# Softmax attention and gated GLU on one core: scores issued as jobs of one head and one key tile, in an order from an event model

## The chip, the cores and the metric

The kernel runs on one core of a Trainium2 chip. The metric is device time in microseconds: 1281.01 us before, the median of three runs (1276.12 to 1281.82). Engines: TensorE (PE, with its weight loads as PEld), VectorE (DVE), ScalarE (ACT), GpSimd (POOL), and SyncE (SP), which issues most DMAs.

## What is computed

x is 2048 x 640, in bf16. After a LayerNorm, 32 heads of width 20 attend over all 2048 tokens, and a GLU of inner width 1728 makes a gate for the result.

```python
    def _A_ref(x, wqkv, wo):
        B, S, D = x.shape
        H = 32; Dh = D // H
        qkv = (lambda x, *d: x.transpose(*d))((x @ wqkv).reshape(B, S, 3, H, Dh), 2, 0, 3, 1, 4)
        q, k, v = qkv[0], qkv[1], qkv[2]
        scale = Dh ** -0.5
        scores = jnp.einsum("bhqd,bhkd->bhqk", q, k) * scale
        p = _softmax(scores, axis=-1)
        o = jnp.einsum("bhqk,bhkd->bhqd", p, v)
        return (lambda x, *d: x.transpose(*d))(o, 0, 2, 1, 3).reshape(B, S, D) @ wo
    ...
    x = A_x
    xn = _layernorm(x, axis=-1)
    s = _A_ref(xn, A_wqkv, A_wo)
    g = _silu(_B_ref(xn, B_w_gate, B_w_up, B_w_down))
    return x + s * g
```

`_B_ref` is sigmoid(xn @ w_gate) * (xn @ w_up), times w_down.

## The kernel before

**Lead.** Four chunks of 512 tokens are normalised (statistics on VectorE, L217 to L223, the scaling on ScalarE, L227), transposed on TensorE (L232) into `xnT`, and K of the first head group is projected (L240, L241). After the fourth chunk the largest K is found over 2048 tokens (L136); then come the first Q and two of the six V pieces of the first pair of groups (L242 to L250).

**Blocks.** The rest is 32 blocks: 8 groups of 4 heads, times 4 chunks of 512 queries. A block has 16 key tiles times 4 heads, 64 score tiles of 128 keys x 512 queries, one PSUM bank each. 12 key tiles (`AKT`) go to ScalarE, which takes the exp of two heads in one instruction of two banks into a `pt` buffer (L549, L550; 6 buffers). 4 key tiles (`DKT`) go to VectorE, which builds the exponential in integers: one instruction clears two banks of `scD` to `iv` (L559), and four passes over `iv` make four tables `pb` (L567), each with its own scaled V (`vss`, made on GpSimd, L173). The four heads lie in four 32-row strips of TensorE, so score matmuls of different heads run side by side; PV matmuls (L456) write 21 rows for each head into strips of the one bank `oacc`. A PV round is four matmuls, one for each head: 12 + 4 x 4 = 28 rounds a block.

**PSUM.** Two slots `scA` of 2 banks, `scD` of 2, `oacc` 1, and one bank `misc` for all else: K, Q and V of the coming group, and the GLU (`item_k`, `item_q`, `item_v`, `item_gu`, `item_down`), at the end the output projection (`item_out`).

**Order.** The order on TensorE, ScalarE and VectorE is the program's own (`manual_schedule`); each engine runs its queue in that order. One step of the loop (L538) is one exp. After it come the VectorE instructions put off from earlier steps (`deferred`), the fill of the slot two steps ahead, and then either, on even steps, the matmuls of one whole step of an item (five for a projection), or up to four PV rounds from one queue over all heads. `norm` (L462) follows the last PV round of a block: VectorE copies `oacc` (L465), SyncE sends the sums to DRAM and back as `lt` (L467, L469), VectorE takes the reciprocal (L471) directly behind the copy in its queue, then `rd`, four broadcasts `rl`, GpSimd's product `on_bf` (L478) and the stores to `oU`. GLU items run in the first 28 blocks, output items (chunk by chunk, when a chunk of queries has gone through all groups) in the last three and behind the loop.

Of the kernel before, what the change touches and what calls it, by code (L numbers as in the profile page):

```python
# [18 lines left out]
P = 128  # L19
# [31 lines left out]
def kernel(  # L51
# [25 lines left out]

    def exp_act(o, i):
        zero = mybir.ImmediateValue(dtype=FP32, value=0.0)
        sc = mybir.ImmediateValue(dtype=FP32, value=exp_scale)  # L80
        return nc.scalar.add_instruction(mybir.InstActivation(  # L81
            func=ACT.Exp, name=nc.get_next_instruction_name(), engine=ENG.Activation,
            ins=[nc.scalar.lower_ap(i), zero, sc, zero], outs=[nc.scalar.lower_ap(o)]))
# [47 lines left out]
    def k_evac(ps, g, c):  # L131
        nc.vector.tensor_scalar(out=kTs[g % 2][:, c * 512:(c + 1) * 512], in0=ps,
                                scalar1=ones_r[:, 0:1], scalar2=None, op0=ALU.add)
        if c == S // 512 - 1:
# [29 lines left out]
    def v_evac(ps, pr, tts, eng=None):  # L164
# [3 lines left out]
        for i, tt in enumerate(tts):  # L168
            if tt in DKT:
                vf = wk.tile([P, 2 * GC], FP32, tag="vf", bufs=1, name="vf")  # L170
# [9 lines left out]
    with tc.tile_pool(name="ln", bufs=2) as lp, \  # L180
# [29 lines left out]

        for c in range(NQC):
# [8 lines left out]
            nc.scalar.activation(out=rstd, in_=mv[:, :, 1:2], func=ACT.Sqrt, bias=eps_t, scale=1.0)  # L220
            nc.vector.reciprocal(out=rstd, in_=rstd)
# [4 lines left out]
            for i in range(4):  # L226
                nc.scalar.activation(out=xn[:, i, :], in_=xt[:, i, :], func=ACT.Identity,  # L227
                                     bias=nb[:, i, :], scale=rstd[:, i, :])
            for kd in range(KD):
                tp = psP.tile([P, 4 * P], BF16, tag="tp", bufs=3, name="tp")  # L230
# [4 lines left out]
                if kd % 2 == 0:  # L235
                    nc.vector.tensor_copy(out=dst, in_=tp)
                else:
                    nc.scalar.copy(out=dst, in_=tp)
# [398 lines left out]
```

## Time and profile before

| | before |
|---|---|
| median of the runs | 1281.01 us |
| profiled execution | 1271.02 us |
| its span | 1269.3 us |
| TensorE busy | 975.9 us (77%) |
| VectorE busy | 867.4 us (68%) |
| ScalarE busy | 807.5 us (64%) |
| GpSimd busy | 98.7 us (8%) |
| DMA | 54.63 MB, mean 43 GB/s |
| mean granted TensorE clock | 0.887 |

The rows further down come from one profiled execution. Times are in us from the start of its span, unless marked ns. Matmuls are pipelined and their ends are modelled, so that TensorE's need is better read from the distance of starts than from its busy time. A wait is written as "who waited <- for whom". [...]

### The profile page before, as it was taken

What the parts mean: (1) busy time and instruction counts of PE and PEld (TensorE: products, weight loads), DVE (VectorE), ACT (ScalarE), POOL (GpSimd) and SP (SyncE); (2) the same over time, 40 slices, a digit from 0 to 9 for tenths busy, and PEclk for the clock granted to TensorE, in tenths of its full rate; (3) what the DMA queues carried; (4) which work ended last, traced back from release to release, by engine and by line L of the source; (5) the groups of instructions that cost most, each with busy time, mean ns of one, the idle gap of its engine ahead of it and who ended that gap; (6) DMA issues with size and microseconds to landing.
All of it is one profiled execution on the core that took longest, in us unless ns stands there. A gap on an engine that the chain in (4) does not pass through costs nothing. (4 is left out here: it accounts for less than half of the span.)

```text
span 1269.3 us, 19838 instructions
## 1 busy us (share of the span) xinstructions
PE 975.9 (77%) x7552; PEld 343.1 (27%) x7552; DVE 867.4 (68%) x1654; ACT 807.5 (64%) x918; POOL 98.7 (8%) x144
## 2 busy tenths in 40 slices
PE   4787787777877777877778778777877877777874
PEld 2322222323222222332222222332222222222222
DVE  6767776666756676667666766766775767577871
ACT  6567765556666666665577676656675766776750
POOL 2100000110000000011000000000100000002223
PEclk9889988889889898988899898889898998978885
DMA  6311111011121110001111110010111000002323
GB/s 174 103 47 38 41 38 34 23 32 47 33 53 34 28 48 27 19 23 30 51 31 34 41 38 25 17 31 24 53 33 28 13 22 27 19 14 73 95 76 105
DMA packets 85808, 54.63 MB, mean 43 GB/s; under 512 B 33552, under 2 KB 79440, under 8 KB 85712
## 3 DMA queue, kind: packets, MB, share of 16 engines
q1 hardware_dynamic: 84560, 52.05, 14.9%
q8 instruction: 59, 0.97, 0.3%
q10 hardware_dynamic: 1152, 1.31, 0.3%
q14 instruction: 37, 0.30, 0.1%
HBM read 42.32 MB, written 8.39 MB: 40 GB/s over the span
## 5 line engine op out<-in xcount | busy, mean ns | idle before, releaser
L81 ACT ACTIVATE pt<-scA_461 128x1024 bf16<-128x1024 f32 x384 | 397.0, 1034 | 232.0 <-PE oacc L456 223.7
L81 ACT ACTIVATE pt<-scA_462 128x1024 bf16<-128x1024 f32 x384 | 396.7, 1033 | 105.1 <-PE scA_462 L434 61.5
L567 DVE TENSOR_SCALAR pb<-iv 128x1024 int16<-128x1024 int16 x1024 | 383.5, 437 | 45.8 <-PE oacc L456 39.0
L559 DVE TENSOR_SCALAR iv<-scD 128x1024 int16<-128x1024 f32 x256 | 311.5, 1217 | 19.2 <-PE scD L434 18.6
L321 PE MATMUL mps<-xnT,wgu 128*128 128x512 bf16 (+1 forms) x560 | 155.5, 413 | 54.7 <-DVE hT L343 44.3
L434 PE MATMUL scA_461<-q,kT_70 32*128 32x512 bf16 x384 | 81.1, 415 | 47.0 <-ACT pt L81 46.8
L434 PE MATMUL scA_461<-q,kT_69 32*128 32x512 bf16 x384 | 77.6, 397 | 49.5 <-ACT pt L81 48.5
L434 PEld LDWEIGHTS <-kT_69 32*128 32x128 bf16 x1024 | 45.6, 91 | 204.6 <-issue 200.7
L434 PEld LDWEIGHTS <-kT_70 32*128 32x128 bf16 x1024 | 44.9, 92 | 198.9 <-issue 194.6
L478 POOL TENSOR_TENSOR on_bf<-on,rl 128x512 bf16<-128x512 f32 x32 | 41.8, 1307 | 712.4 <-DMA rl<-rd 636.6
L471 DVE RECIPROCAL rt<-lt 128x16 f32<-128x16 f32 x32 | 8.1, 253 | 122.9 <-DMA lt<-ld 122.9
L321 PEld LDWEIGHTS <-wgu 128*128 128x128 bf16 (+1 forms) x560 | 52.4, 103 | 128.2 <-issue 91.5
L434 PE MATMUL scA_462<-q,kT_70 32*128 32x512 bf16 x384 | 82.6, 426 | 5.3 <-ACT pt L81 5.0
L456 PE MATMUL oacc<-pt,v_72 128*21 128x512 bf16 x768 | 74.0, 404 | 16.1 <-DVE on L465 16.1
L355 PE MATMUL mps<-wd,hT 128*128 128x320 bf16 x448 | 77.6, 308 | 10.7 <-DVE gqs L371 10.1
L434 PE MATMUL scA_462<-q,kT_69 32*128 32x512 bf16 x384 | 79.1, 407 | 5.4 <-ACT pt L81 5.0
L456 PE MATMUL oacc<-pt,v_71 128*21 128x512 bf16 x768 | 70.5, 392 | 13.4 <-DVE on L465 13.4
L343 DVE SCALAR_TENSOR_TENSOR hT<-tnh,mps 128x512 bf16<-128x512 bf16 (+1 forms) x56 | 38.4, 685 | 60.7 <-PE mps L321 59.7
L456 PE MATMUL oacc<-pb,vs_74 128*21 128x512 bf16 x768 | 73.2, 433 | 0.0
L333 ACT ACTIVATE tnh<-mps 128x512 bf16<-128x512 f32 (+1 forms) x56 | 33.5, 599 | 60.3 <-PE mps L321 60.3
L456 PE MATMUL oacc<-pb,vs_73 128*21 128x512 bf16 x768 | 70.3, 417 | 0.0
L161 PE MATMUL mps<-wv,xnT 128*128 128x160 bf16 x290 | 34.5, 293 | 34.1 <-DVE vf L171 26.5
(84 smaller groups left out, 826.1 us busy)
## 6 DMA issues: line engine op xcount, KB each, us to landing
rl<-rd SPq DMA_DIRECT2D x128, 64.0 KB
wgu<-in_B_w_gate_dram SPq DMA_DIRECT2D x24, 320.0 KB
wgu<-in_B_w_up_dram SPq DMA_DIRECT2D x24, 320.0 KB
gq_dram<-gqs SPq DMA_DIRECT2D x32, 160.0 KB
gqr<-gq_dram SPq DMA_DIRECT2D x16, 320.0 KB
xr<-in_A_x_dram SPq DMA_DIRECT2D x16, 160.0 KB
out_dram<-ot SPq DMA_DIRECT2D x16, 160.0 KB
oU<-on_bf SPq DMA_DIRECT2D x112, 20.0 KB
```

The lines of the kernel that those rows point to most:

```text
L81: return nc.scalar.add_instruction(mybir.InstActivation(func=ACT.Exp, name=nc.get_next_instruction_name(), engine=ENG.Activation, ins=[nc. ...
L161: nc.tensor.matmul(ps[:, i * 2 * GC:(i + 1) * 2 * GC], lhsT=xnT[:, kd, tt * P:(tt + 1) * P], rhs=w[:, kd, :], start=(kd == 0), stop=(kd == ...
L321: nc.tensor.matmul(ps[0:fs, :], lhsT=w[:, i, kd, ko * P:ko * P + fs], rhs=xnT[:, kd, c * QC:(c + 1) * QC], start=(kd == 0), stop=(kd == KD ...
L333: nc.scalar.activation(out=st["t"][0:fs, :], in_=st["g"][0:fs, :], func=ACT.Tanh, scale=0.5)
L343: nc.vector.scalar_tensor_tensor(out=hT[0:fs, kf, :], in0=st["t"][0:fs, :], scalar=1.0, in1=st["u"][0:fs, :], op0=ALU.add, op1=ALU.mult)
L355: nc.tensor.matmul(st["ps"][:, 0:HD], lhsT=hT[0:fsz[kf], kf, t4 * P:(t4 + 1) * P], rhs=wd[0:fsz[kf], kf, h * HD:(h + 1) * HD], start=(kf = ...
L434: nc.tensor.matmul(sc[:, i, :], lhsT=kTs[(b_ // NQC) % 2][32 * j:32 * j + 32, kt_ * P:(kt_ + 1) * P], rhs=qs[b_][32 * j:32 * j + 32, :], s ...
L456: nc.tensor.matmul(oacc[32 * j:32 * j + DH + 1, :], lhsT=lhsT, rhs=rhs, start=(i == 0), stop=(i == tot - 1), tile_position=(0, 32 * j), sk ...
L471: nc.vector.reciprocal(out=rt, in_=lt)
L478: nc.gpsimd.tensor_tensor(out=on_bf, in0=on, in1=rl, op=ALU.mult)
L559: nc.vector.tensor_scalar(out=iv, in0=scD, scalar1=I_OFF, scalar2=I_LOW, op0=ALU.add, op1=ALU.max)
L567: nc.vector.tensor_scalar(out=pb[:, k, :, :].bitcast(I16), in0=iv, scalar1=0.25, scalar2=cst, op0=ALU.mult, op1=ALU.add)
```

## The change

The unit of work becomes a job: one head and one key tile, one bank of scores. ScalarE has a slot of three banks and one of two, filled and read in turn; VectorE has a slot of one bank, and its `iv` and `pb` tiles now hold all four heads of a key tile, so that clearing takes four instructions of 512 columns and a pass is one of 2048. `pt` becomes 3 buffers of 3 jobs and 4 of 2 (17 jobs where there were 12), `pb` 2 of 4 heads (3 of 2 before). Jobs are claimed when a slot is filled; when the ScalarE key tiles of a block are used up, ScalarE takes VectorE's that nobody has begun (`claim_act`).

The order comes from a small model that runs while the program is written: it keeps the time at which each engine is free, with fixed lengths for each kind of instruction, and issues on each engine the next thing that its model holds ready. On TensorE a fill goes first when ScalarE would starve, projections are issued matmul by matmul (M), and PV as rounds of one unit from each head's own queue; K, Q and V items go before GLU and output items. `norm` is cut in two: `norm_a` copies `oacc` and sends the sums, `norm_b` with the reciprocal is issued at least 7 us of model time later.

Smaller edits: half of the LayerNorm scaling goes to GpSimd, every K chunk has its own maximum (`k_max`), K evacuation in the lead is on ScalarE, the first Q is projected after the first chunk, the exp table is loaded by an exp after the last square root, all six V pieces of the first pair move into the loop, and the buffers of the output stage share the place of the GLU's down weights (`wd`). Tanh takes its scale as an immediate. The score, projection, evacuation and PV instructions are otherwise as before. Behind the loop `norm_b` of the last block and the output items that are left are issued in sequence.

Its core:

```diff
+    def k_evac(ps, g, c, on_act=False):
+        dst = kTs[g % 2][:, c * 512:(c + 1) * 512]
+        if on_act:
+            nc.scalar.activation(out=dst, in_=ps, func=ACT.Identity, bias=ones_r[:, 0:1], scale=1.0)
+        else:
+            nc.vector.tensor_scalar(out=dst, in0=ps, scalar1=ones_r[:, 0:1], scalar2=None, op0=ALU.add)
+
+    def k_max(g, c):
+        if c == 0:
+            mks[g] = wk.tile([P, NQC], FP32, tag="mk4", bufs=2, name="mk4")
+        nc.vector.tensor_reduce(out=mks[g][:, c:c + 1], in_=kTs[g % 2][:, c * 512:(c + 1) * 512],
+                                axis=AXISX, op=ALU.max, apply_absolute_value=True)
+        if c == NQC - 1:
             mk = wk.tile([P, 1], FP32, tag="mk", bufs=2, name="mk")
-            nc.vector.tensor_reduce(out=mk, in_=kTs[g % 2], axis=AXISX, op=ALU.max,
-                                    apply_absolute_value=True)
+            nc.vector.tensor_reduce(out=mk, in_=mks[g], axis=AXISX, op=ALU.max)
...
             k_mm(psk, 0, c)
-            k_evac(psk, 0, c)
-        psq = psP.tile([P, 512], FP32, tag="pq", bufs=1, name="psq")
-        q_mm(psq, 0, 0)
-        aq0 = q_abs(psq)
+            k_evac(psk, 0, c, on_act=True)
+            k_max(0, c)
...
-    scA = [psum.tile([P, 2, 512], FP32, name=f"scA{i}", tag=f"scA{i}") for i in range(2)]
-    scD = psum.tile([P, 2, 512], FP32, name="scD", tag="scD") if ND else None
+    SLOT = (3, 2)
+    scA = [psum.tile([P, n, 512], FP32, name=f"scA{n}", tag=f"scA{n}") for n in SLOT]
+    scD = psum.tile([P, 512], FP32, name="scD", tag="scD")
     oacc = psum.tile([P, QC], FP32, name="oacc", tag="oacc")
     nc.vector.memset(oacc, 0.0)
...
+    LAT = 0.07
+    D_WAIT = 0.0
+    T_F, T_PV, T_MM, T_MODE = 0.215, 0.216, 0.216, 0.10
+    T_IV, T_PASS, T_ON = 0.655, 0.63, 0.66
+    NPT, NPB, NIV = (3, 4), 2, 2
+
+    def t_exp(n):
+        return 0.095 + 0.4267 * n
...
+    def claim_act(n):
+        got = []
+        for b in range(min(NBLK - 1, claimed[0] // NJOB), NBLK):
+            while len(got) < n and (a_left[b] or d_left[b]):
+                if q_at.get(b, 1e9) > now:
+                    return got
+                if not a_left[b]:
+                    kt = d_left[b].pop()
+                    a_left[b] = [(kt, j) for j in range(GH)]
+                kt, j = a_left[b].pop(0)
+                if any(x[2] == j for x in got):
+                    a_left[b].insert(0, (kt, j))
+                    return got
+                got.append((b, kt, j))
+                claimed[0] += 1
+            if len(got) == n:
+                break
+        return got
+
+    def claim_dve():
+        for b in range(claimed[0] // NJOB, min(NBLK, claimed[0] // NJOB + 2)):
+            if d_left[b]:
+                if q_at.get(b, 1e9) > now:
+                    return None
+                claimed[0] += GH
+                return b, d_left[b].pop(0)
+            if a_left[b]:
+                return None
+        return None
...
+    def pv_pick(j):
+        for u in pv_q[j]:
+            if u["b"] == pv_block[0] and u["ready"] <= now and v_at.get((u["b"] // NQC // 2, u["kt"]), 1e9) <= now:
+                return u
+        return None
...
         on = w2.tile([P, QC], FP32, tag="on", bufs=2, name="on")
         nc.vector.tensor_copy(out=on, in_=oacc)
...
+            if free["ACT"] <= now:
+                it = next((e for e in evs if e.i < len(e.ops) and e.ops[e.i][0] == "ACT" and e.ready <= now), None)
+                s = slots[nexp % 2]
...
+                elif s["full"] is not None and s["at"] <= now and buf_free(pt_left[nexp % 2], NPT[nexp % 2]):
+                    jobs = s["full"]
+                    i = nexp % 2
+                    pt = w2.tile([P, SLOT[i], QC], BF16, tag=f"pt{i}", bufs=NPT[i], name=f"pt{i}")
+                    m = len(jobs)
+                    exp_act(pt[:, 0:m, :], scA[i][:, 0:m, :])
+                    end = now + t_exp(m)
+                    free["ACT"] = end
+                    pt_left[i].append([m, 0.0])
+                    for x, (b, kt, j) in enumerate(jobs):
+                        add_unit(b, kt, j, pt[:, x, :], None, end + LAT + 0.1, (pt_left[i], len(pt_left[i]) - 1))
+                    s["full"] = None
+                    s["at"] = end + LAT
+                    nexp += 1
...
+                if norm_pending is not None and norm_pending[1] <= now:
+                    b = norm_pending[0]
+                    on, lt = norm_a(b)
+                    free["DVE"] = now + T_ON
+                    oacc_at[0] = now + T_ON + LAT
+                    timed.append((now + T_ON + 7.0, b, on, lt))
+                    norm_pending = None
...
+                elif tm is not None:
+                    timed.remove(tm)
+                    norm_b(*tm[1:])
+                    o_at[tm[1]] = now + 11.0
+                    free["DVE"] = now + 0.25
+                elif dslot["full"] is not None and dslot["at"] <= now:
+                    d, j = dslot["full"]
+                    nc.vector.tensor_scalar(out=d["iv"][:, j, :], in0=scD, scalar1=I_OFF, scalar2=I_LOW,
+                                            op0=ALU.add, op1=ALU.max)
+                    end = now + T_IV
+                    free["DVE"] = end
+                    dslot["full"] = None
+                    dslot["at"] = end + LAT
+                    d["n"] += 1
+                    if d["n"] == GH:
+                        dve_pass.append(d)
+                elif dve_pass and (dve_pass[0]["k"] > 0 or buf_free(pb_left, NPB)):
...
+                    passes(d["iv"], d["pb"], k)
+                    d["k"] += 1
+                    end = now + T_PASS
+                    free["DVE"] = end
+                    for j in range(GH):
+                        add_unit(d["b"], d["kt"], j, d["pb"][:, k, j, :], k, end + LAT + 0.1, d["rel"])
...
+            if free["PE"] <= now:
+                s = slots[nfill % 2]
+                can_f = s["full"] is None and s["at"] <= now
+                starve = max(0.0, free["ACT"] - now) + sum(t_exp(len(x["full"])) for x in slots if x["full"])
+                us = [u for u in map(pv_pick, range(GH)) if u is not None] if oacc_at[0] <= now else []
+                n_ready = min(sum(u["ready"] <= now and u["b"] == pv_block[0] for u in q) for q in pv_q)
+                forced = not all(buf_free(pt_left[i], NPT[i]) for i in range(2)) or not buf_free(pb_left, NPB)
+                pv_ok = len(us) == GH or (len(us) > 0 and (forced or pv_all(pv_block[0])))
+                m_ok = (cur is not None and cur.ops[cur.i][0] == "PE" and cur.ready <= now) if (
+                    cur is not None and cur.i < len(cur.ops)) else False
+                nxt = None
+                stay = (mode == "M" and m_ok) or (mode == "PV" and pv_ok)
+                d_idle = dslot["full"] is None and dslot["at"] <= now and not dve_pass and free["DVE"] <= now + 0.4
+                next_f = slots[nfill % 2]["at"] if slots[nfill % 2]["full"] is None else free["ACT"] + LAT
+                if can_f and (starve < 0.75 or not stay):
+                    nxt = "F"
+                elif d_idle and (can_f or next_f > now + D_WAIT) and (dcur is not None or buf_free(iv_left, NIV)):
+                    nxt = "F"
+                elif mode == "M" and m_ok:
+                    nxt = "M"
+                elif mode == "PV" and pv_ok:
+                    nxt = "PV"
+                elif pv_ok and (n_ready >= 3 or not m_ok):
+                    nxt = "PV"
+                elif m_ok:
+                    nxt = "M"
+                elif pv_ok:
+                    nxt = "PV"
+                if nxt == "F":
+                    jobs = claim_act(SLOT[nfill % 2]) if can_f else []
+                    todo = [(scA[nfill % 2][:, x, :],) + t for x, t in enumerate(jobs)]
...
+                            js = [j for j in dcur["left"] if j not in busy_j]
+                            if js:
+                                dcur["left"].remove(js[0])
+                                todo.append((scD, dcur["b"], dcur["kt"], js[0]))
+                                d_new = (dcur, js[0])
+                                if not dcur["left"]:
...
+                    if todo:
+                        dur = T_F + (T_MODE if mode != "F" else 0.0)
+                        for t in todo:
+                            score_mm(*t)
...
+                if nxt == "M":
+                    op = cur.ops[cur.i]
+                    if step == 0 and op[1] is not None:
+                        op[1]()
+                    dur = op[2][step][0] + (T_MODE if mode != "M" else 0.0)
+                    op[2][step][1]()
+                    step += 1
+                    free["PE"] = now + dur
...
+                elif nxt == "PV":
+                    dur = T_PV + (T_MODE if mode != "PV" else 0.0)
+                    b = pv_block[0]
+                    pv_emit(us, now + dur + 0.1)
+                    free["PE"] = now + dur
+                    mode = "PV"
+                    if pv_all(b) and pv_units[b] == 0:
+                        norm_pending = (b, now + dur + LAT + 0.1)
+                        oacc_at[0] = 1e9
+                        pv_block[0] += 1
+            now += STEP
```

## Rows read from the trace of the kernel before

**Rows 1.** Stretches: lead, main loop, block 28's undisturbed part, tail.

```profile
core 0: us, PE busy (x) PEld busy (x) DVE busy (x) ACT busy (x) POOL busy (x), PEclk, DMA share, GB/s
0.00:39.60 39.60, 19.18 (x136) 11.15 (x137) 27.32 (x79) 20.20 (x30) 8.46 (x29) 0.96 0.67 188
39.60:1233.10 1193.50, 941.61 (x7362) 325.10 (x7362) 833.92 (x1563) 787.27 (x888) 79.80 (x104) 0.89 0.13 37
1109.90:1135.10 25.20, 21.25 (x166) 5.22 (x166) 21.65 (x42) 18.83 (x22) 1.27 (x1) 0.74 0.05 15
1233.10:1269.30 36.20, 15.12 (x55) 6.84 (x53) 6.17 (x13) 0.00 (x0) 10.49 (x13) 0.58 0.33 98
```

**Rows 2.** Longest waits of PE, ACT and DVE, 80 to 1233 us.

```profile
engine line waited for: us in total, times, longest us
ACT pt L81 <- PE oacc L456: 217.5, 101, 3.7
...
DVE rt L471 <- DMA lt<-ld: 119.3, 31, 6.2
...
PE scA_461 L434 <- ACT pt L81: 90.2, 119, 1.2
...
ACT tnh L333 <- PE mps L321: 60.3, 15, 6.0
...
PE mps L321 <- DVE hT L343: 44.3, 13, 5.1
```

**Rows 3.** Timeline around the normalisation at 619 us: start, length, engine, line, count, [idle].

```profile
619.39 0.68 DVE L465 COPY on<-oacc 128x512 f32<-128x512 f32 x1
...
626.31 0.25 DVE L471 RECIPROCAL rt<-lt 128x16 f32<-128x16 f32 x1 [6.25 <-DMA lt<-ld]
...
628.50 2.29 PE L321 MATMUL mps<-xnT,wgu 128*128 128x512 bf16 x5 [4.03 <-DVE hT L343]
```

**Rows 4.** Timeline of TensorE at full clock, 601 to 604 us.

```profile
601.59 0.39 PE L434 MATMUL scA_461<-q,kT_70 32*128 32x512 bf16 x2 [0.95 <-ACT pt L81]
...
601.92 1.25 PE L321 MATMUL mps<-xnT,wgu 128*128 128x512 bf16 x5
...
603.10 0.39 PE L434 MATMUL scA_462<-q,kT_70 32*128 32x512 bf16 x2
...
603.42 0.40 PE L456 MATMUL oacc<-pt,v_72 128*21 128x512 bf16 x4
...
603.75 0.39 PE L434 MATMUL scA_461<-q,kT_70 32*128 32x512 bf16 x2
```

**Rows 5.** Timeline at low clock, 1116 us: a score fill, then a PV round.

```profile
1116.26 0.61 PE L434 MATMUL scA_461<-q,kT_70 32*128 32x512 bf16 x2
...
1116.80 0.61 PE L456 MATMUL oacc<-pt,v_72 128*21 128x512 bf16 x4
```

**Rows 6.** Timeline of ScalarE, 1123 us: two exps back to back.

```profile
1123.32 1.02 ACT L81 ACTIVATE pt<-scA_462 128x1024 bf16<-128x1024 f32 x1
...
1124.22 1.03 ACT L81 ACTIVATE pt<-scA_461 128x1024 bf16<-128x1024 f32 x1
```

**Rows 7.** Groups by line and form: busy us, mean ns.

```profile
L567 DVE TENSOR_SCALAR pb<-iv 128x1024 int16<-128x1024 int16 x1024 | 383.5, 437 | 45.8 <-PE oacc L456 39.0
...
L559 DVE TENSOR_SCALAR iv<-scD 128x1024 int16<-128x1024 f32 x256 | 311.5, 1217 | 19.2 <-PE scD L434 18.6
...
L155 DVE TENSOR_SCALAR q<-mps 128x512 bf16<-128x512 f32 x31 | 21.1, 680 | 3.3 <-PE mps L151 2.9
...
L333 ACT ACTIVATE tnh<-mps 128x512 bf16<-128x512 f32 x52 | 31.2, 599 | 51.7 <-PE mps L321 51.7
...
L227 ACT ACTIVATE xn<-xt,nb,rstd 128x640 bf16<-128x640 bf16 x16 | 13.5, 911 | 2.7 <-DVE nb L223 2.7
...
L478 POOL TENSOR_TENSOR on_bf<-on,rl 128x512 bf16<-128x512 f32 x32 | 41.8, 1307 | 712.4 <-DMA rl<-rd 636.6 <-DVE iv L559 75.3 <-POOL vs_73 L173 0.3
```

**Rows 8.** Timeline, end of the lead.

```profile
35.16 2.29 DVE L136 TENSOR_REDUCE mk<-kT_69 128x1 f32<-128x2048 bf16 x1
...
40.08 1.28 ACT L81 ACT_TABLE_LOAD   x1 [7.45 <-PE scD L434]
```

More of the change, by code (lines that the diff above doesn't have):

```diff
@@ L265, in misc_ps @@
     def misc_ps():
[L266 to L300 removed]
+        return psum.tile([P, 512], FP32, tag="misc", bufs=1, name="mps")
     wgu_tiles = {}
@@ new lines, in mk_k, with alloc, k_mm1 @@
+    def mk_k(g, c, at):
+        st = {}
+        def alloc():
+            st["ps"] = misc_ps()
+        mms = [lambda kd=kd: k_mm1(st["ps"], g, c, kd) for kd in range(KD)]
+        return Item([("PE", alloc, [(T_MM, f) for f in mms]),
+                     ("DVE", 0.66, lambda: k_evac(st["ps"], g, c), "free"),
+                     ("DVE", 0.66, lambda: k_max(g, c))], at, prio=0)
+    def k_mm1(ps, g, c, kd):
+        nc.tensor.matmul(ps, lhsT=wslice(g, 1, kd), rhs=xnT[:, kd, c * 512:(c + 1) * 512],
+                         start=(kd == 0), stop=(kd == KD - 1))
@@ new lines, with add_unit @@
+    pv_q = [[] for _ in range(GH)]
+    pv_jobs = {}
+    pv_units = {b: 0 for b in range(NBLK)}
+    pv_started = {}
+    pv_block = [0]
+    oacc_at = [0.0]
+    pt_left = [[], []]
+    pb_left = []
+    def add_unit(b, kt, j, src, k, ready, rel):
+        if k is None or k == NB - 1:
+            pv_jobs[(b, j)] = pv_jobs.get((b, j), 0) + 1
+        pv_q[j].append(dict(b=b, kt=kt, j=j, k=k, src=src, ready=ready, rel=rel))
+        pv_units[b] += 1
+    def pv_pick(j):
[3 more added lines that the diff above has]
+        return None
@@ new lines, in pv_all, with pv_emit @@
+    def pv_all(b):
+        return all(pv_jobs.get((b, j), 0) == TT for j in range(GH))
+    def pv_emit(us, end):
+        for u in us:
+            b, kt, j, k = u["b"], u["kt"], u["j"], u["k"]
+            pr, go = divmod(b // NQC, 2)
+            pv_q[j].remove(u)
+            pv_units[b] -= 1
+            first = not pv_started.get((b, j))
+            pv_started[(b, j)] = True
+            last = pv_jobs.get((b, j), 0) == TT and not any(x["b"] == b for x in pv_q[j])
+            if not k:
@@ L590 @@
-        for m in sorted(deferred):
-            for fn in deferred[m]:
-                fn()
-        while pv_queue:
-            _, b_, kt_, k_ = pv_queue.pop(0)
-            pv_round(b_, kt_, k_)
-        while pe_steps:
-            pe, ev = pe_steps.pop(0)[:2]
-            pe()
-            if ev is not None:
-                ev()
-        for t4 in range(4):
-            for h in range(2):
-                for pe, ev, _ in item_out(4 * (NQC - 1) + t4, h):
-                    pe()
-                    if ev is not None:
-                        ev()
+            if cur is None and misc_at <= now:
+                can = [x for x in items[:80] if x.at <= progress() and (
+                    x.need is None or o_at.get(x.need, 1e9) <= now)]
+                cur = min(can, key=lambda x: x.prio) if can else None
@@ L610 @@
+        for tm in timed:
+            norm_b(*tm[1:])
+        for it in items + [mk_out(4 * (NQC - 1) + t4, h, 0.0) for t4 in range(4) for h in range(2)]:
+            for op in it.ops:
+                if op[0] == "PE":
+                    if op[1] is not None:
+                        op[1]()
+                    for _, f in op[2]:
+                        f()
+                else:
+                    op[2]()
 _INS = ['A_x', 'A_wqkv', 'A_wo', 'B_x', 'B_w_gate', 'B_w_up', 'B_w_down']
```

521 lines of the change are left out of this document (291 added, 230 removed).

## The prediction

> **What bounds the kernel now.** Read the stretches first [rows 1]. The profiled execution took 1271.02 us: 1269.3 us of span and 1.7 around it. The lead up to the first score matmul is 39.6 us, the 32 attention blocks 1193.5, the tail 36.2. The loop is 94% of the time, 1193.5 / 32 = 37.3 us a block, and in it no engine is full: VectorE 833.9 us (70%), ScalarE 787.3 (66%). TensorE's 941.6 (79%) is a modelled figure, so I work its need out below from starts. The loop is therefore bound by the order in which work stands in the queues, and the next view is who waits for whom [rows 2]. Three patterns carry it. ScalarE waits 217.5 us, 101 times, for PV matmuls: an exp has no free `pt` buffer, because the PV that would free one stands further back in TensorE's queue. VectorE waits 119.3 us, about 3.8 a block, at the reciprocal of the normalisation for a DMA. TensorE waits at a score fill for an exp (90.2 us, 119 times), or at a projection for the one `misc` bank (44.3 us, 13 times). The third view, the timeline after one such reciprocal, shows how one feeds the next [rows 3]: the copy of `oacc` at 619.39, the reciprocal only at 626.31 after 6.25 us idle, behind it the GLU evacuation, and TensorE at 628.50 after 4.03 us of waiting for that, with fills behind it.
>
> **What each engine needs after the change.** *ScalarE.* Two exps of 1024 columns start 0.90 us apart at a length of 1.02 [rows 6]; 512 columns take 0.60 [rows 7]. A bank more is thus about 1.02 - 0.60 = 0.42 us. The 3-bank exp is not in this trace; from below it costs 1.5 x 0.90 = 1.35 less all of its fixed part, from above 1.35. I take 0.90 + 0.42 = 1.32. Five jobs cost 1.32 + 0.90 = 2.22 us where they cost 2.25, so 1536 jobs save some 10 us (0 to 20), and 787 becomes 777. The wide slot brings next to nothing on the engine itself; what it brings is the fifth bank of scores in flight.
>
> *VectorE.* 256 bank pairs `iv` at 1.217 become 512 single ones: at least 0.608 each (pure columns), at most 0.68 (the nearest 512-column read of PSUM) [rows 7]. I take 0.66: 338 us for 311. The 1024 passes take 383.5 / 1024 = 0.375 each when they follow each other. Of the 512 passes of double width that take their place none is in the trace: at most 0.75, and at least 0.50, if they save as much as the shortest instruction shown (the 0.25 reciprocal [rows 3]). I take 0.62: 317 for 384. The K maximum split in four adds up to 8 us, I take 4; two V evacuations come over from the lead, 2 us. So 834 + 27 - 66 + 6 = 801 (about 710 to 840).
>
> *The claim rule.* ScalarE takes a VectorE key tile when its own are used up. A tile is 4 x (0.66 + 0.62) = 5.1 us on VectorE and 4 x 0.444 = 1.8 on ScalarE, so 801 - 5.1n = 777 + 1.8n gives n = 3.5 in the whole kernel and 783 us, **24.5 us a block** for both. With VectorE at 710, ScalarE alone bounds at 24.3; at 840 it is 24.8. The unknown prices hardly move this bound.
>
> *TensorE at full clock.* From starts [rows 4]: a fill to the first projection matmul 0.32; five projection matmuls to the next fill 1.18; fill to PV 0.32; one PV round to a fill 0.33. That is 0.22 for each round or matmul and 0.10 for each change of kind. A block needs 48 / 2.5 = 19.2 fills with a change before and after each, 19.2 x 0.42 = 8.1; 28 PV rounds, 6.2; by the code 886 matmuls of 512 columns, 608 of 320 and 320 of 160 in the whole kernel, at 0.216 and in proportion to columns 191 + 82 + 22 = 295, 9.2 a block; some 9 more changes, 0.9. Sum **24.4 us**, as much as the other two. [...]
>
> **How full the engines get.** The nearest stretch is 1109.9 to 1135.1, in the one block without GLU, K or output work and behind its reciprocal [rows 1]: there score fills and PV alternate much as the new order would have them, and VectorE is busy 0.86, TensorE 0.84, ScalarE 0.75 of it. I take the middle one, 0.84, because after the change all three need the same: 24.5 / 0.84 = 29.17 us a block, 933 for 32. The ends are 0.80 and 0.90: 980 and 871.
>
> **The stalls and where they go.** The reciprocal moves at least 7 us behind the copy by the model; the trace needs 0.68 for the copy and on average 3.8 behind it, 6.9 in all at 619 [rows 2, 3], so it should mostly find its data, and the 119 us go. SyncE then runs `ld` and `lt`, whatever GLU loads and stores were issued meanwhile, and then `rd`, four `rl` and the `oU` stores, 7 us later than now; nobody in the loop waits for these but GpSimd's `on_bf`, with the V scalings queued behind it, and the output items from block 29 on. The pt wait is met by 17 jobs of buffers for 12 and by PV rounds that are picked as soon as four heads are ready; next late is then whichever of the three engines is behind. GLU, K, V and Q keep one `misc` bank; that costs nothing while fills and PV cover the evacuation, and up to the 44 us of [rows 2] if not. The output buffers in `wd`'s place wait for the last down matmul of block 27; their first use is in block 29, so nothing.
>
> **Lead and tail.** In the lead the table load of 1.28 us comes before the first exp's data, and of the 2.29 us maximum only a quarter stands before the last Q [rows 8]: -3.0. Half of the normalisations go to GpSimd; the nearest rows are 0.91 on ScalarE and 1.31 for 512 elements on GpSimd [rows 7], so a chunk's four take between 2 x 0.91 and 2 x 1.64 instead of 3.6: a gain, but one that the DMA-fed statistics may hide. Lead 36.6 (33 to 43). The tail keeps its chain: 36.2 (up to 45, should slices of the one output tile wait for each other).
>
> **Sum** on the profiled execution: 36.6 + 933 + 36.2 + 1.7 = 1007.5 us. The median of the runs, 1281.01, is 1.0079 times the profiled 1271.02, so **1015 us**.
>
> **The rivals.** [...]
>
> *Only the reciprocal's wait goes.* The order misses in the rest: 37.3 - 3.7 = 33.6, again 1159. This is the case in which the event model does not do what it says.
>
> *Better packing.* 0.93, half way from 0.86 to full: 26.3 a block, 916, or 923 us. For it: ScalarE ran gapless at 0.90 spacing around 1123 with TensorE at full clock.
>
> *Slower: the fixed order is wrong by one exp.* The order is decided by modelled times, and real queues keep it. If the model thinks ScalarE ahead by w, TensorE stands w before each fill, with PV and projections stuck behind it: 24.4 + 19.2w. From w = 0.67 us this is as slow as now; with the 90.2 / 119 = 0.76 that a waiting fill waits today it is 39.0 a block, 1322, or 1333 us. Against: only 119 of the 384 fills of that slot wait so now, and a late engine delays the others too, which brings the order back. [...]
>
> **How the numbers follow.** Forecast 0.50, low clock 0.19, only the reciprocal 0.11, better packing 0.09, slower 0.08, no change 0.03. Half a per cent is about what a measurement can tell from no change. Faster by more: 0.89; within: 0.03; slower: 0.08. The forecast's own range is 945 to 1075 (0.90 and 0.80, lead and tail at their ends). The range of 930 to 1175 leaves out most of better packing, the upper parts of the two cases at 1159, no change and slower.
>
> **What would show it.** Right: blocks of 28 to 31 us between copies of `oacc`; DMA waits at the reciprocal under 20 us in all; exp waits for PV under 60; the three engines each over 0.78 in the loop; granted clock over 0.95; about 614 exps. [...] The slow case shows as hundreds of fill waits for an exp near 0.7. The forecast is wrong if the busy sums of VectorE or ScalarE rise above 840, or if waits of one kind over 150 us remain.

## The result and the profile after

965.42 us, the median of three runs (961.33 to 975.89), against 1281.01 before: a ratio of 0.7528 (95% interval 0.7471 to 0.7586). The forecast was 1015 us. The execution that was profiled took 965.42 us too, with a span of 963.7. All ratios in this document leave out the executions over 1.5% above the fastest of the same kernel: 975.89 here, and further down two of the four each of the kernel with two-bank slots and of the first one with fewer PV rounds, so that the medians of these three read 2 to 9 us too high beside their ratios.

The stretches of the kernel after, lead, loop and tail, in the columns of [rows 1]:

```profile
0.00:38.75 38.75, 15.90 (x104) 8.83 (x106) 21.78 (x72) 19.79 (x32) 14.07 (x34) 0.96 0.60 154
38.75:873.10 834.35, 798.14 (x6899) 268.34 (x6985) 725.11 (x1188) 778.98 (x749) 66.66 (x85) 0.99 0.16 44
873.10:963.70 90.60, 53.77 (x282) 29.59 (x281) 21.18 (x44) 4.09 (x9) 26.54 (x33) 0.87 0.45 135
```

| us | before | forecast | after |
|---|---|---|---|
| lead | 39.6 | 36.6 | 38.8 |
| loop | 1193.5 | 933 | 834.4 |
| a block | 37.3 | 29.2 | 26.1 |
| tail | 36.2 | 36.2 | 90.6 |

So the total is nearer to the forecast than its parts: the loop came out 99 us shorter and the tail 54 longer. In the loop TensorE is now busy 0.96 of the time, ScalarE 0.93 and VectorE 0.87, at a granted clock of 0.99 (1.00 is full speed in the traces, and the one other level that those of both kernels list is 0.50). The first number of the x columns shows the other half: 282 projection matmuls stand behind the loop where 55 stood before.

The longest waits of the three engines in the loop (engine, line, waited for: us, times, longest), to be laid beside [rows 2]:

```profile
DVE iv L747 <- PE scD L540: 85.9, 160, 1.4
...
ACT pt_5422 L81 <- PE oacc L580: 5.0, 1, 5.0
...
PE scD L540 <- DVE iv L747: 3.6, 8, 0.8
...
DVE rt L603 <- DMA lt<-ld: 0.7, 1, 0.7
```

The reciprocal's 119.3 us are 0.7. The exps' 217.5 us for PV are 9 waits with 25.6 us in all, the longest of 5.0. What is left is VectorE waiting 160 times for a fill of its one-bank slot.

Groups by line and form of VectorE in the loop (busy us, mean ns, idle before), for [rows 7]:

```profile
L747 DVE TENSOR_SCALAR iv<-scD 128x512 int16<-128x512 f32 x452 | 310.0, 686 | 95.4 <-PE scD L540 85.9 <-PE scA_429 L540 5.8 <-PE scA_428 L540 1.5
L625 DVE TENSOR_SCALAR pb<-iv 128x2048 int16<-128x2048 int16 x452 | 307.9, 714 | 3.0
...
L168 DVE TENSOR_SCALAR q<-mps 128x512 bf16<-128x512 f32 x31 | 21.1, 682 | 0.4 <-PE mps L164 0.4
```

452 instead of 512: ScalarE took 15 of VectorE's 128 key tiles. And ScalarE's timeline in the middle of the loop (start, length, engine, line), for [rows 6]:

```profile
600.84 1.15 ACT L81 ACTIVATE pt_7841<-scA_429 128x1024 bf16<-128x1024 f32 x1
601.88 1.45 ACT L81 ACTIVATE pt_7869<-scA_428 128x1536 bf16<-128x1536 f32 x1
603.23 1.02 ACT L81 ACTIVATE pt_7880<-scA_429 128x1024 bf16<-128x1024 f32 x1
604.14 1.46 ACT L81 ACTIVATE pt_7895<-scA_428 128x1536 bf16<-128x1536 f32 x1
605.47 1.04 ACT L81 ACTIVATE pt_7924<-scA_429 128x1024 bf16<-128x1024 f32 x1
```

From 601.88 on the starts are 1.35, 0.91 and 1.33 us apart: no idle time.

The tail's timeline shows down items and then output items, each waiting for the evacuation of the one before:

```profile
883.73 2.17 PE L425 MATMUL mps<-wd,hT 128*128 128x320 bf16 x14 [1.05 <-DVE gqs L435]
...
885.93 0.44 ACT L81 ACTIVATE td<-mps 128x320 bf16<-128x320 f32 x1 [2.77 <-PE mps L425]
886.40 0.49 DVE L435 SCALAR_TENSOR_TENSOR gqs<-td,mps 128x320 f32<-128x320 bf16 x1 [2.73 <-ACT td L81]
886.95 2.17 PE L425 MATMUL mps<-wd,hT 128*128 128x320 bf16 x14 [1.05 <-DVE gqs L435]
...
911.37 1.49 PE L457 MATMUL mps<-wo,oU 128*128 128x320 bf16 x5 [0.58 <-DVE ob L464]
...
913.50 0.96 PE L457 MATMUL mps<-wo,oU 128*128 128x320 bf16 x3 [0.64 <-DVE ob L464]
...
936.41 0.84 PE L457 MATMUL mps<-wo,oU 128*128 128x320 bf16 x5 [0.65 <-DVE ob L464]
...
937.89 0.84 PE L457 MATMUL mps<-wo,oU 128*128 128x320 bf16 x5 [0.64 <-DVE ob L464]
```

A down item takes 3.2 us (883.73 to 886.95), an output item 2.1 (911.37 to 913.50) where the granted clock has a mean of 0.52 (911 to 924 us) and 1.5 where it is 1.00 (936.41 to 937.89). The GLU had not come round in time: the code behind the loop issues whatever items are left, not only output items, and the last unit, all eight down items of the last chunk and all 32 output items are run here, one after the other through the single `misc` bank.

### The profile page after: what moved, and what is told of

Its sections match the earlier page's. It is cut to its first block, busy times and chain, and to the rows that moved or that the text cites. A ratio compares the mean times of both kernels' runs of the same rounds, so it can differ in the third digit from the quotient of the medians.

```text
span 963.7 us, 18399 instructions
## 1 busy us (share of the span) xinstructions
PE 867.8 (90%) x7285; PEld 306.8 (32%) x7372; DVE 768.1 (80%) x1302; ACT 802.9 (83%) x790; POOL 107.3 (11%) x152
## 4 chain that ended last, share of the span: by engine, by line
PE 49%; ACT 24%; DVE 18%; issue 5%; DMA 3%; POOL 1%; SPq 0%; POOLq 0%; DVEq 0%; another core or an unknown queue 0%; ACTq 0%
PE oacc L580 13%; PE mps L402 10%; DVE pb L625 7%; PE scA_428 L540 6%; PE mps L425 5%; DVE iv L747 5%; PE scA_429 L540 5%; PE scD L540 4%; PE mps L457 2%; PE mps L372 2%; PE mps L341 1%; DVE ob L464 1%; PE mps L352 1%; DMA ob<-gq_dram 1%; DVE hT L410 1%
## 5 line engine op out<-in xcount | busy, mean ns | idle before, releaser
L747 DVE TENSOR_SCALAR iv<-scD 128x512 int16<-128x512 f32 x452 | 310.0, 686 | 95.4 <-PE scD L540 85.9
L625 DVE TENSOR_SCALAR pb<-iv 128x2048 int16<-128x2048 int16 x452 | 307.9, 714 | 3.0
L402 PE MATMUL mps<-xnT,wgu 128*128 128x512 bf16 (+1 forms) x505 | 150.9, 385 | 7.7 <-DVE hT L410 1.4
L540 PE MATMUL scD<-q,kT_69 32*128 32x512 bf16 x228 | 87.9, 385 | 2.3 <-DVE iv L747 1.8
L425 PE MATMUL mps<-wd,hT 128*128 128x320 bf16 x448 | 80.9, 306 | 8.6 <-DVE gqs L435 7.5
L540 PE MATMUL scD<-q,kT_70 32*128 32x512 bf16 x224 | 85.6, 382 | 2.1 <-DVE iv L747 1.8
L580 PE MATMUL oacc<-pb,vs_74 128*21 128x512 bf16 x684 | 80.2, 382 | 1.7 <-DVE pb L625 1.2
L580 PE MATMUL oacc<-pb,vs_73 128*21 128x512 bf16 x672 | 79.7, 382 | 1.6 <-DVE pb L625 1.3
L540 PEld LDWEIGHTS <-kT_70 32*128 32x128 bf16 x1024 | 38.5, 91 | 123.4 <-issue 119.4
L540 PEld LDWEIGHTS <-kT_69 32*128 32x128 bf16 x1024 | 39.2, 91 | 120.8 <-issue 113.9
L402 PEld LDWEIGHTS <-wgu 128*128 128x128 bf16 (+1 forms) x560 | 44.1, 98 | 85.1 <-issue 58.4
L540 PE MATMUL scA_428<-q,kT_69 32*128 32x512 bf16 x478 | 64.5, 387 | 7.4 <-DVE q L168 3.2
L540 PE MATMUL scA_428<-q,kT_70 32*128 32x512 bf16 x480 | 64.8, 383 | 4.6 <-ACT pt_2941 L81 0.5
L540 PE MATMUL scA_429<-q,kT_70 32*128 32x512 bf16 x320 | 64.0, 383 | 1.4 <-ACT pt_3070 L81 0.4
L540 PE MATMUL scA_429<-q,kT_69 32*128 32x512 bf16 x318 | 63.3, 386 | 1.4 <-ACT pt_7252 L81 0.5
L425 PEld LDWEIGHTS <-hT 128*128 128x128 bf16 x448 | 38.9, 98 | 49.4 <-issue 37.4
L457 PE MATMUL mps<-wo,oU 128*128 128x320 bf16 x160 | 31.2, 332 | 23.1 <-DVE ob L464 22.1
L464 DVE SCALAR_TENSOR_TENSOR ob<-mps,ob 128x320 f32<-128x320 f32 x32 | 15.7, 492 | 38.2 <-PE mps L457 31.1
L580 PEld LDWEIGHTS <-v_71 128*21 128x21 bf16 x1024 | 27.7, 90 | 41.1 <-issue 33.0
```

What stands on the lines that cost most here:

```text
L402: nc.tensor.matmul(st[key][0:fs, :], lhsT=w[:, i, kd, ko * P:ko * P + fs], rhs=xnT[:, kd, c * QC:(c + 1) * QC], start=(kd == 0), stop=(kd ...
L425: nc.tensor.matmul(st["ps"][:, 0:HD], lhsT=hT[0:fsz[kf], kf, t4 * P:(t4 + 1) * P], rhs=wd[0:fsz[kf], kf, h * HD:(h + 1) * HD], start=(kf = ...
L457: nc.tensor.matmul(st["ps"][:, 0:HD], lhsT=oU[:, kd, tt * P:(tt + 1) * P], rhs=wo[:, kd, h * HD:(h + 1) * HD], start=(kd == 0), stop=(kd = ...
L464: nc.vector.scalar_tensor_tensor(out=tmp, in0=st["ps"][:, 0:HD], scalar=0.25, in1=gqr[:, sl], op0=ALU.mult, op1=ALU.mult)
L540: nc.tensor.matmul(dst, lhsT=kTs[(b // NQC) % 2][32 * j:32 * j + 32, kt * P:(kt + 1) * P], rhs=qs[b][32 * j:32 * j + 32, :], start=True, s ...
L580: nc.tensor.matmul(oacc[32 * j:32 * j + DH + 1, :], lhsT=lhsT, rhs=u["src"], start=first, stop=last, tile_position=(0, 32 * j), skip_group ...
```

## The experiments

The theory: the event model lets a fill go first, so the loop lasts as long as ScalarE and VectorE need for the scores; TensorE gives projections what is left, and what does not fit is done behind the loop, at a higher price. The rivals: TensorE itself sets the loop's pace; or one part of the change alone (the reciprocal, the wide slot, the cut projections) brings nearly all.

**The reciprocal, on the kernel after.** `norm_b` stands right behind the copy of `oacc` again.

```diff
-timed.append((now + T_ON + 7.0, b, on, lt))
+timed.append((now + T_ON, b, on, lt))
...
-                elif it is not None:
+                elif it is not None and tm is None:
```

> The changed kernel with the reciprocal issued directly behind the copy of oacc again, all else as it is. VectorE then stands 3 to 4 us a block, some 110 us, with 109 us of idle time in the loop. If the place of the reciprocal is worth what its wait was before: 1040 to 1075. If TensorE is the bound and the other engines' buffers cover the wait: 965 to 985.

1123.18 us, ratio to before 0.8797 (0.8766 to 0.8829). The loop's stretch, and the wait in question:

```profile
38.35:1029.70 991.35, 875.09 (x7047) 277.54 (x7047) 736.04 (x1199) 788.26 (x750) 67.47 (x85) 0.91 0.14 37
```
```profile
DVE rt L603 <- DMA lt<-ld: 109.9, 31, 5.3
```

The wait of before is back, 3.5 us a block. It costs 158 us in the whole, 157 of them in the loop: 110 of waiting and 47 that come with it. How much of these is the lower clock (0.91 for 0.99) was not separated.

**The reciprocal, on the kernel before.** `norm_b` moves behind the eighth exp.

```diff
+        if step_n[0] + 8 < NW:
+            deferred.setdefault(step_n[0] + 8, []).append(lambda: norm_b(b, on, lt))
+        else:
+            norm_b(b, on, lt)
+
+    def norm_b(b, on, lt):
+        g, c = divmod(b, NQC)
         rt = w2.tile([P, GH * QC // P], FP32, tag="rt", bufs=2, name="rt")
         nc.vector.reciprocal(out=rt, in_=lt)
...
```

> The kernel before with this one part of the change: the reciprocal and what follows it put off by eight exps. As predicted for the case that only this wait goes: 3.7 us a block, 119 us, to 1150 to 1170 (0.905). Rival: the time goes to the next wait (pt buffers, the misc bank) and less than 50 us is gained: 1230 or more.

1140.10 us, ratio 0.8916 (0.8866 to 0.8965). Its loop, and the wait of before that stayed as it was:

```profile
39.48:1112.35 1072.87, 892.12 (x7366) 312.31 (x7366) 832.31 (x1563) 784.17 (x888) 79.53 (x104) 0.94 0.15 41
```
```profile
ACT pt L81 <- PE oacc L456: 213.7, 104, 4.5
```

So the reciprocal alone is 137 us of 316, everything else without it 153 (1276.63 to 1123.18). They add up to 290, so the two are nearly independent, and the reciprocal alone does not bring nearly all.

**The wide slot.** Two slots of two banks; ScalarE then makes 796 exps for 639.

```diff
-    SLOT = (3, 2)
+    SLOT = (2, 2)
...
-    NPT, NPB, NIV = (3, 4), 2, 2
+    NPT, NPB, NIV = (4, 4), 2, 2
```

> Both ScalarE slots of two banks (16 jobs of pt buffers for 17). ScalarE itself loses 10 us by the distance of its starts. If TensorE is the bound, the 128 more exps bring fills with a change of kind before and after each, up to 128 x 0.42 = 54 us: 995 to 1020. If the slot's width does not matter: within 15 us of 965.

1045.30 us, ratio 0.8117 (0.8042 to 0.8192); by the ratios (0.7528 after) that is some 75 us more than after, and more than the 54 that I had expected at most.

```profile
38.73:882.97 844.24, 824.07 (x6837) 255.70 (x6837) 723.02 (x1180) 785.47 (x890) 71.57 (x85) 0.99 0.14 39
882.97:1045.80 162.83, 103.92 (x443) 49.44 (x441) 31.00 (x58) 13.17 (x25) 26.54 (x33) 0.78 0.33 97
```

The loop is only 10 us longer; the tail is 72 longer, with 443 matmuls for 282 (and a clock of 0.78 for 0.87, which has a part in it). ScalarE is hardly busier (785 for 779). What the fifth bank brings is time on TensorE: counted from the starts, 799 rounds of fills became 975, and 1552 changes of kind 1757. At 0.22 and 0.10 these are some 59 us, and the projections that lost their place moved behind the loop.

**The cut projections.** All matmuls of a projection step are issued together.

```diff
-                    dur = op[2][step][0] + (T_MODE if mode != "M" else 0.0)
-                    op[2][step][1]()
-                    step += 1
+                    dur = sum(x[0] for x in op[2]) + (T_MODE if mode != "M" else 0.0)
+                    for x in op[2]:
+                        x[1]()
+                    step = len(op[2])
```

> All matmuls of one step of an item are issued together, as before the change. Theory (cutting keeps ScalarE fed): fills come up to 1.2 us later, 985 to 1040. Rival (cutting only costs changes of kind on the engine that bounds): some 300 changes of 0.10 less, 930 to 955.

959.35 us, ratio 0.7509 (0.7478 to 0.7540): no difference to the kernel after that these intervals can tell.

```profile
38.30:921.08 882.78, 824.35 (x7123) 295.35 (x7124) 715.15 (x1166) 802.09 (x767) 82.25 (x102) 0.98 0.18 50
921.08:958.80 37.72, 21.09 (x73) 9.61 (x71) 7.48 (x17) 0.00 (x0) 13.07 (x16) 0.55 0.40 123
```

But its parts differ: the loop has 48 us more and the tail 53 less. As I read it, whole projections hold up the fills, so the loop is longer and there is room for them in it. Changes of kind fell to 1238, which is 31 us less of TensorE, but the total does not show them: at their median distances TensorE's starts now fill 0.88 of the loop, for 0.92 after. Loop and tail are one account.

**One engine less, the order kept.** Three kernels keep the issue order of after and leave out work: PV rounds of three of VectorE's four tables (TensorE), its fourth pass (VectorE), the third bank of each wide exp (ScalarE).

```diff
-            nc.tensor.matmul(oacc[32 * j:32 * j + DH + 1, :], lhsT=lhsT, rhs=u["src"], start=first, stop=last,
+            if k in (0, None) or first or last:
+                nc.tensor.matmul(oacc[32 * j:32 * j + DH + 1, :], lhsT=lhsT, rhs=u["src"], start=first, stop=last,
...
```

> Leaves out the PV matmuls of VectorE's tables 1 to 3 (only the first and last of a block stay), in the order of the changed kernel; VectorE and ScalarE do all their work. That takes 113 key tiles x 3 = 339 PV rounds of 0.22 us, 75 us, from TensorE and nothing from the others. If TensorE is what bounds the loop of 834 us (798 busy), the time falls by 40 to 75 us, to 890 to 925, until ScalarE (779 busy) is full. If ScalarE or VectorE bounds it, it stays within 15 us of 965.

```diff
-                    passes(d["iv"], d["pb"], k)
+                    if k < NB - 1:
+                        passes(d["iv"], d["pb"], k)
...
```

> Leaves out the fourth pass over iv; PV reads the third table in its place, so TensorE does all its work. VectorE loses 113 x 0.68 = 77 us. If TensorE bounds the loop: within 15 us of 965. If VectorE does: 890 to 930.

```diff
-                    exp_act(pt[:, 0:m, :], scA[i][:, 0:m, :])
+                    e = min(m, 2)
+                    exp_act(pt[:, 0:e, :], scA[i][:, 0:e, :])
...
```

> The exp of the 3-bank slot takes only two banks, and PV reads the second bank for the third job. ScalarE loses some 320 x 0.42 = 135 us of 779. If TensorE bounds the loop: within 15 us of 965. If ScalarE does: 880 to 930.

972.67, 974.21 and 958.31 us (ratios 0.7556, 0.7608, 0.7528; intervals of ±0.007 to 0.010). Their loops, in this order:

```profile
38.47:871.27 832.80, 765.27 (x5671) 259.33 (x5746) 727.22 (x1188) 776.21 (x749) 66.10 (x85) 0.99 0.16 43
```
```profile
38.92:868.65 829.73, 797.38 (x6899) 267.40 (x6985) 657.70 (x1075) 778.14 (x749) 66.27 (x85) 0.99 0.16 44
```
```profile
39.16:867.14 827.98, 795.51 (x6899) 261.28 (x6985) 723.62 (x1188) 675.62 (x749) 67.73 (x85) 0.99 0.16 44
```

67 us less on VectorE or 103 less on ScalarE shorten the loop by 5 and 6 us; fewer PV rounds by 2. (What their times differ by lies in the tails, with the same 282 matmuls in 102.9, 104.7 and 88.6 us at clocks of 0.67, 0.65 and 0.90.) With the order fixed none of the three bounds alone: they alternate in it, and an engine that is done sooner waits for the next entry of another: VectorE with its fourth pass left out waits 136.6 us for its fills, where it waited 85.9. That doesn't tell the theory from its rival, so the next two let the model know.

**Less work, and the model knows.** First TensorE: the PV rounds of two tables are not queued at all.

```diff
+        if k in (1, 2):
+            left, i = rel
+            left[i][0] -= 1
+            return
         pv_q[j].append(dict(b=b, kt=kt, j=j, k=k, src=src, ready=ready, rel=rel))
```

> Leaves out the PV rounds of VectorE's tables 1 and 2, and the event model knows it, so that the order is made for the lighter TensorE: 226 rounds of 0.22 = 50 us less, and some changes of kind. In the frozen order no engine's relief moved the time. If TensorE's total bounds loop and tail together, the freed time takes in items that now wait for the tail: 890 to 920, with fewer matmuls behind the loop (282 now). If the frozen order was not the reason and the dependences bound the loop: within 15 us of 965.

Then ScalarE and VectorE: fourth pass and third bank are left out, and their times are too.

```diff
-                        end = now + T_PASS
+                        end = now + (T_PASS if k < NB - 1 else 0.0)
...
-                    end = now + t_exp(m)
+                    end = now + t_exp(e)
...
```

> Leaves out the fourth pass over iv (77 us of VectorE) and the third bank of each wide exp (some 135 us of ScalarE), and the event model knows both, so that the order is made for them. If TensorE bounds: within 15 us of 965, the loop shorter and the tail longer by as much. If ScalarE and VectorE bound the loop: 860 to 910 with the tail as it is.

922.20 us (0.7214, 0.7177 to 0.7252) and 997.65 (0.7806, 0.7760 to 0.7852). Loop and tail of the one and the other:

```profile
38.52:878.48 839.96, 787.05 (x6192) 271.31 (x6264) 731.05 (x1201) 783.18 (x760) 78.96 (x97) 0.99 0.18 49
878.48:927.00 48.52, 28.33 (x95) 13.17 (x94) 9.94 (x21) 0.00 (x0) 16.98 (x21) 0.50 0.48 145
```
```profile
37.49:781.58 744.09, 704.85 (x6389) 226.15 (x6463) 582.38 (x938) 657.07 (x743) 68.21 (x85) 1.00 0.14 38
781.58:1004.00 222.42, 140.50 (x621) 66.94 (x623) 40.87 (x74) 21.32 (x40) 26.57 (x33) 0.85 0.31 92
```

This tells them apart. Lighten TensorE, and the loop stays (+6 us) while the tail loses 42, with 95 matmuls for 282. The 187 others went through the same single `misc` bank in the loop, so that this bank was not what kept them out. Lighten the other two, and the loop loses 90 us, yet the kernel gets 32 slower, since 621 matmuls are left behind it. These 339 more cost 132 us in the tail, 0.39 each, where a projection matmul of 512 columns takes 0.22 in the loop. (With its new times the model also deals the work otherwise: 98 key tiles go to VectorE, for 113 after.) The other two set the pace of the loop; TensorE's sum, and how tightly the loop packs it, sets loop and tail together. Whether ScalarE or VectorE alone, with the order remade, would do the same was not run.

**A wrong length in the model.** The exp is taken 0.25 us too short in the model, and nothing else is edited.

```diff
-        return 0.095 + 0.4267 * n
+        return 0.095 + 0.4267 * n - 0.25
```

> The event model takes each exp as 0.25 us shorter than it is; no instruction changes. It is the prediction's slower case at a known error: if TensorE then stands before each fill with all else behind it, some 640 x 0.25 = 160 us, 1080 to 1130. If a late engine delays the others and the order stays good: under 1000.

1125.20 us, ratio 0.8772 (0.8723 to 0.8822), 160 more than after. The loop, the tail, the fills' wait and VectorE's share of the work:

```profile
36.97:904.54 867.57, 741.50 (x6375) 253.67 (x6444) 638.98 (x1021) 793.54 (x746) 66.84 (x85) 0.99 0.12 33
904.54:1131.00 226.46, 145.10 (x614) 67.85 (x618) 40.14 (x73) 21.08 (x40) 26.47 (x33) 0.81 0.30 87
```
```profile
PE scA L540 <- ACT pt L81: 96.8, 300, 0.8
```
```profile
L747 DVE TENSOR_SCALAR iv<-scD 128x512 int16<-128x512 f32 x384 | 264.5, 689 | 187.2 <-PE scD L540 184.0
```

Fills do wait for exps as the slower rival had it, 300 times, but the loop is only 33 us longer. Even these need not be the waits. The order is not the only thing that changed, as the expectation had it: with exps that look cheap the claim rule gives ScalarE 32 of VectorE's key tiles instead of 15 (384 `iv` for 452), 68 jobs or, at 0.444 each, some 30 us of ScalarE. The run does not separate the two. The tail is 136 longer: a model that thinks its exps shorter sees less room for projections. (639 x 0.25 is 160 as well; that the two agree was not tested with another size.)

**The tail.** First the tail's items rotate over the six banks of the score slots, with six output buffers for two; then, in the last kernel, over eight separate one-bank tiles of a new PSUM pool that is opened when the loop's is closed. The loop is the same in both.

```diff
     def misc_ps():
+        if tail:
+            banks = [scA[0][:, i, :] for i in range(3)] + [scA[1][:, i, :] for i in range(2)] + [scD[:, :]]
+            ring[0] += 1
+            return banks[ring[0] % len(banks)]
...
```

> Behind the loop the items left over take turns on the six banks of scA and scD in place of one misc bank, and output tiles on six buffers in place of two; the loop is unchanged. Theory: the tail of 90.6 us is a chain through one bank (3.21 us for each of 8 down items, 1.49 to 2.14 for each of 32 output items); with six banks TensorE needs 1.9 and 0.7, GpSimd 0.79 an output item, so 8 x 1.9 + 32 x 0.79 + some 10 = 50 us: 920 to 930 in all. Rival: the tail is bound by the output's DMAs (16 tiles, two loads and a store each, about 3 us a tile): not below 955.

944.42 us, 0.7394 (0.7339 to 0.7449). The tail, and four down items in it that go to `scD` and then to the three banks of one tile in turn (the last line holds a fifth item too, in the other tile):

```profile
871.61:941.00 69.39, 45.90 (x279) 27.54 (x277) 20.93 (x43) 4.09 (x9) 25.87 (x33) 0.95 0.52 164
```
```profile
882.66 2.60 PE L432 MATMUL scD<-wd,hT 128*128 128x320 bf16 x14
...
885.20 2.18 PE L432 MATMUL scA<-wd,hT 128*128 128x320 bf16 x14
...
888.42 2.17 PE L432 MATMUL scA<-wd,hT 128*128 128x320 bf16 x14 [1.04 <-DVE gqs L442]
...
891.63 4.28 PE L432 MATMUL scA<-wd,hT 128*128 128x320 bf16 x28 [1.05 <-DVE gqs L442]
```

The tail fell from 90.6 to 69.4 us and not further: matmuls still waited, 1.04 us here, for the read of another bank, where that bank belongs to the same tile, and not where the tile changes.

```diff
     def misc_ps():
+        if tail:
+            return tail[0].tile([P, 512], FP32, tag="t", bufs=8, name="tps")
...
+        pool_stack.close()
+        tail.append(ctx.enter_context(tc.tile_pool(name="psT", bufs=1, space=bass.MemoryType.PSUM)))
```

> As the run with six banks behind the loop, but with eight separate one-bank tiles from a pool of their own, opened when the loop's is closed. Theory: there the matmuls still waited for reads of another bank of the same tile (1.04 us before a down item); with separate tiles a down item costs TensorE's 2.0 and an output item GpSimd's 0.79: the tail of 69 falls to about 50, 920 to 930 in all. Rival: the down items' chain through ScalarE and VectorE or the output DMAs hold it: 940 or more.

**935.93 us** (934.52 to 936.85), ratio 0.7313 (0.7288 to 0.7338): faster than both kernels. Its tail in two stretches, and one line of TensorE's timeline in the first:

```profile
873.04:894.33 21.29, 19.23 (x122) 11.28 (x123) 4.80 (x11) 3.65 (x8) 1.27 (x1) 1.00 0.39 118
894.33:934.80 40.47, 25.20 (x161) 16.45 (x160) 14.24 (x33) 0.44 (x1) 24.28 (x32) 0.82 0.71 218
```
```profile
879.31 15.09 PE L430 MATMUL tps<-wd,hT 64*128 64x320 bf16 x99 [1.40 <-DVE hT L415]
```

99 down matmuls now run without a stop, 0.152 us each, and 29 us of the tail are gone. Some 12 of them lie before the first output item (33.1 us in the kernel after, up to 906.22, for 21.3), where the banks are what differs and the granted clock was 0.90 for 1.00 here. The other 17 lie in the output items (57.5 us for 40.5), where banks and output buffers changed together and were not separated. I had expected some 10 us more; the output part still takes 40.5, in which GpSimd is busy 24.3 and the DMA engines 0.71, so there the loads, sums and stores of the output buffers are probably late next; no run tests that.

## Why the prediction was right, and where it was not

*What held.* The reading that the loop was bound by the order of the queues, with the reciprocal [rows 3] and the `pt` buffers [rows 2] as its main stalls. The exps: forecast 1.32 and 0.90 us apart, 1.33 to 1.35 and 0.91 measured. ScalarE's sum, 777 to 783, was 779 in the loop, 24.3 us a block where the bound was 24.5; but that is in part luck, since by the prediction's own formula the 15 key tiles that it took over would have made it 777 + 15 x 1.8 = 804. The reciprocal's wait under 20 us, the exps' waits under 60, the clock over 0.95: it is 0.99 in the loop where it was 0.89, and 0.91 in the kernel that has the reciprocal's wait back; what lowers it no run separates. So the low clock, 0.19 of the chances and one of the two cases at 1159, is out; no run shows its 1159 us. The price of 0.10 for a change of kind: medians of all starts in the loop are 0.22 from PV to PV and 0.32 from fill to PV or back, at 1552 changes where the working has some 1517 (32 x (2 x 19.2 + 9)).

*What was luck.* The forecast of 1015 us is 5% from the measured time because two misses of opposite sign meet in it, a loop forecast 99 us too long and a tail 54 too short; the blocks of 28 to 31 us that were to show it right came out at 26.1. The lead gained 0.9 us of the 3.0 forecast; no run shows why. (From its own terms the forecast's range is 949 to 1078, not 945 to 1075; nothing hangs on that.)

*Mis-sized: the packing.* The loop took 26.1 us a block, not 29.2. That is 24.5 / 26.1 = 0.94 for 0.84, the size of the rival that I gave 0.09. The nearest stretch [rows 1, third line] was one of the old order with its own waits left in it, and at a granted clock of 0.74 its TensorE share was no measure for the clock of 1.00 that the forecast took (fill to PV is 0.54 us at 0.50 and 0.32 at 1.00 [rows 5, 4]); an order that interleaves three engines by their modelled times leaves fewer. TensorE's starts say the same: at their medians they sum to some 770 us of 834, 0.92.

*Mis-sized, without weight: VectorE.* `iv` 0.686 for 0.66, just above the upper bound that was taken from [rows 7]; the pass 0.681 for 0.62, so that the double width saves 0.07 us on 2 x 0.375. The range "about 710 to 840" was too narrow as well: its upper prices, 0.68 and 0.75, give 834 + 37 + 6 = 877. Fifteen tiles went to ScalarE, not 3.5, and 452 of each at these prices are 618 us, with which VectorE was no bound. 86 us of its time it waits for fills, and part of TensorE's rounds are made for it alone: 799 rounds of fills where I had 614.

*The step that failed: "the tail keeps its chain: 36.2".* It took for granted that all projections fit into the loop. I had TensorE's need, 24.4 us a block, and the room only in the forecast's 29.2. With the real rounds it is the 770 us of the loop and some 39 behind it (8 x 14 + 160 matmuls of 320 columns at 0.136, ten of 512 at 0.216), 809 or 25.3 a block; in blocks of 26.1 with a packing of 0.92 that doesn't go in. So the better-packing rival, which has the loop right, has the sum wrong too, with its 923: each us that the loop gains for lack of waiting is one less for projections, and each projection behind the loop is dearer (0.39 us for 0.22 in the kernel with the two lighter engines). The kernels with slots of two banks, with whole projections and with lighter engines all move work between the two, and the one with separate banks shows a part of the price: 29 us of the tail were the single bank and the two output buffers.

*The rivals.* "Only the reciprocal" (1159 us) is what the old kernel with a late reciprocal measured, 1140; the rest of the change brings as much again. The slower case was right that the model's lengths matter, w = 0.25 cost 160 us where it has 19.2 x 0.25 x 32 = 154; but its place was wrong: mostly not in fills that wait in the loop but in projections that come behind it, so that the agreement of the two sums is chance as far as is known.

*Weight loads.* In the kernel after, projection matmuls of 512, 320 and 160 columns (L402, L425, L372) that follow each other start 0.216, 0.136 and 0.069 us apart in the median, in proportion to their columns, though each has a weight load of 128 columns, of 0.097, 0.099 and 0.101 us in the mean. So the loads are hidden, as in the five of [rows 4], also at 0.216; in the down item at 883.73 each load is recorded while a matmul runs. The 0.152 of the 99 down matmuls in the last kernel is a mean over items: one item follows the other in 2.11 us, 12 steps of 0.136 and two, to the 64-row piece of the weights and from it, that take 0.48 together.

## What to carry to other kernels

Where an issue order lets the critical work go first, the filler is not free: add up the engine that does both, for the loop and for what is left at its end, and give the leftovers their own resources (here separate PSUM banks and more output buffers, 29 us). A wait on a round trip through DMA at the head of an in-order queue cost more than its length here, 158 us for 110, and moving it back by some microseconds was nearly independent of the rest of the order. And an order made from modelled times is as good as its lengths: 0.25 us on one instruction lost half of what the change had won.

## What was not expected of the hardware

Writing a bank waited for the reads of another bank of the same PSUM tile, as this program's semaphores have it, and not where the banks are tiles of their own: waits of 1.04 us between down items against none, and tails of 69.4 and 61.8 us with the same work, in six banks and in eight. Doubling the width of the `pb` pass saved 0.07 us of 0.75, so that this pass is nearly all columns. And seven of the loops shown here, with quite different work, have TensorE busy between 0.93 and 0.98: a full engine in the table of busy shares did not mean that it set the pace.
